# Attention rounds two at a time, the weight fold begun earlier, and copies written in the order of their target

## The chip, the cores and the metric

The kernel runs on one NeuronCore of a Trainium2 chip. The metric is the time of one execution on the device, in microseconds (us). Five engines work side by side, each with its own queue in order: TensorE (matmuls into PSUM), VectorE, ScalarE, GpSimd, and SyncE, whose queue here issues all DMA transfers. A matmul has two rows in a trace: the load of its weights (PEld) and the matmul itself (PE).

## The reference

Inputs come as float64. First an attention with a window: batch 4, 8 heads, 576 tokens, head size 64. Then two MLPs on the 2304 tokens of width 512.

```python
scores = scale * np.matmul(q, k.transpose(0, 1, 3, 2))
rel = pos[:, None] - pos[None, :]
mask_plain = (rel >= 0) & (rel < 32)
mask_dil = (rel >= 0) & (rel < 128) & (rel % 4 == 0)   # heads 4 to 7; heads 0 to 3 have mask_plain
attn = softmax(where(mask, scores, -1e9))
x = (attn @ v) as 2304 x 512
h = x @ w_in; x = maximum(0.01 * h, h) @ w_out         # 512 -> 2048 -> 512
a = x @ w1; b = x @ w2                                 # 512 -> 1024
out = ((a * b) @ w3) @ w_out2                          # 1024 -> 1024 -> 512
```

## The kernel before

**Numbers.** q, k and v are float32; the weights arrive as float64 words, and three engines make float32 of them (`to_float32`, lines 144 to 158: a scaling on a chosen engine, two on ScalarE, a shift and a sum on VectorE). For the MLPs each operand is split in a high and a low part (`split`), and a product is three matmuls (`mm3`, lines 118 to 122).

**Attention.** Two heads make a pair; a pair is worked in two rounds (320 and 256 queries), 8 rounds a batch, 32 in all. A round has these stages. `scores`: per block of 64 queries two 64x64 matmuls against 96 keys, which lie together in the dilated heads because q and k are turned in that order; then scale and mask, the maximum (VectorE), an exponential per block (ScalarE). `normalize`: reciprocal (VectorE) and product (GpSimd). `turn_p`: the probabilities are transposed on TensorE and copied to SBUF by ScalarE. `value_steps`: matmuls with v, then a cast of the result into `x` (ScalarE, line 500) and the low part (VectorE, line 503). In the dilated heads the result goes to every fourth token of `x`. q and k of batch 0 are turned on TensorE and copied by `turn_rows` (line 374), those of batches 1 to 3 on VectorE (`turn_halves`). Two PSUM banks ("side") serve scores, probabilities and values.

**First MLP.** The tokens are in 7 chunks (`CH`), four of 320 or 256 tokens and three of 384. A turn (c, f) is one of 16 slices of 128 hidden columns: `hidden_steps` has 12 matmuls into one of two "h" banks, then a prelu on ScalarE (line 563), which frees the bank, and a split; `project` (12 matmuls) follows two turns later.

**Order.** The first stretch, batches 0 and 1 with the conversion of w_in and w_out and the first 36 turns, stands in an order written out by hand (the string `START`). After it the order of each engine is made by a planner that goes by the program's order and simulated times. There `attention(16, 32)` is a generator, the stream, for batches 2 and 3. After each turn's hidden matmuls `pace` takes some steps of it: 39/28 a turn in chunks 2 and 3, 2.25 a turn from the beginning of chunk 4 (counted from 0) to its turn 13. A round has four steps: `turn_p(n)` with `normalize(n + 1)`; `scores(n + 2)`; the turn of one q or k and a load of another; `value_steps(n)`, after some rounds with a load of v.

**Fold.** At turn 13 of chunk 4 (`LATE`) the rest of the stream is issued, the attention's memory (pool `att`) is closed, and a pool `fold` is opened in its place. `fold_step` converts w_out2 (8 jobs) and w3 (16 jobs) and forms w3 @ w_out2 on TensorE, 1.35 steps a turn through chunk 5. During chunk 6, the last, w1 and w2 are converted, and the product of the fold is loaded back (`load_wp`) and split.

**End.** The second MLP: gates (`gate`) and the last product (`final`).

Of the kernel before, what the change touches and what calls it, by code (L numbers as in the profile page):

```python
# [22 lines left out]
DILATION = 4  # L23
# [5 lines left out]
def tile_window_attention_two_mlps(  # L29
# [70 lines left out]
    def copy_on(e):  # L100
        return e.copy if e is nc.scalar else e.tensor_copy
# [152 lines left out]
    def load_halves(m, src, o):  # L254


        pi, nm = seq[m // 2], "qk"[m % 2]
        t = att.tile([P, NT, D], F32, tag="nat", name=f"{nm}{pi}", bufs=2)
        for g in range(P // E):
            og = o + g // 2 * S * D + g % 2 * E  # L260
            to = t[g * E : (g + 1) * E]
            x = NT * D - E
            nc.sync.dma_start(
                to.rearrange("p n d -> p (n d)")[:, :x], rows(src, og, [[NT * D, E], [1, x]])
            )
        nat_t[nm, pi] = t

    def turn_halves(m):
        pi, nm = seq[m // 2], "qk"[m % 2]
        t = nat_t.pop((nm, pi))  # L270
        dst = att.tile([P, S], F32, tag=nm + "T", name=f"{nm}T{pi}", bufs=2)
        if pair(pi)[2]:
            nc.vector.transpose(dst.rearrange("d (r n) -> d n r", n=NT), t[:, :, :E])
        else:
            for v in range(DILATION):
                us = len(range(v, NT, DILATION))
                other = (NT + v) % DILATION * SR + (NT + v) // DILATION
                to = bass.AP(
                    dst.tensor, dst.offset + v * SR,
                    [list(dst.ap[0]), [1, us], [2 * NT // DILATION, E // 2], [other - v * SR, 2]],  # L280
                )
                at = bass.AP(
                    t.tensor, t.offset + v * D,
                    [list(t.ap[0]), [DILATION * D, us], [2, E // 2], [1, 2]],
                )
                nc.vector.transpose(to, at)
        qk_t[nm, pi] = dst
# [69 lines left out]
    def turn_rows(m):  # L357
        pi, nm = seq[m // 2], "qk"[m % 2]
        plain = pair(pi)[2]
        c = 6 if plain else 8  # L360
        n = S // c
        t = nat_t.pop((nm, pi))
        ps = bank2(f"ps_{nm}T{pi}")
        for g in range(2):
            for c1 in range(c // 2):
                src = t[:n, g * (c // 2) + c1].rearrange("p j d -> p (j d)")
                nc.tensor.transpose(ps[:, g, c1 * n : (c1 + 1) * n], src, ident[:n, :n])
        yield
        dst = att.tile([P, S], F32, tag=nm + "T", name=f"{nm}T{pi}", bufs=2)
        if plain:  # L370
            to = dst.rearrange("d (p g c) -> d g c p", g=2, p=n)
        else:
            to = dst.rearrange("d (c p g) -> d g c p", g=2, p=n)
        copy_on(engine_of[TURN_ON[m]])(to, ps[:, :, : S // 2].rearrange("d g (c p) -> d g c p", p=n))
        qk_t[nm, pi] = dst
        yield

# [2 lines left out]
    def scores(n):  # L380
        if n < NR:
            run(score_steps(n))
# [76 lines left out]
    def value_steps(n):  # L459

        pi, r = order[n]
        b, hp = divmod(pi, HP)
        t = pt.pop(n)
        nb = t.shape[1]
        ps = side_bank(f"ps_o{n}")[:, : nb * QB]
        b, hp = divmod(pi, HP)
        plain = pair(pi)[2]
        vt = v_t[4 * b + 2 * plain + r]
        h = 2 * (hp % (HP // 2))
        for i in range(nb):  # L470
            for j in range(2):
                nc.tensor.matmul(  # L472
                    ps[j * D : (j + 1) * D, i * QB : (i + 1) * QB],
                    vt[i][:, h + j, :],
                    t[:, i, j * QB : (j + 1) * QB],
                    start=True, stop=True,
                )
        yield
        x = xs[hp][:, :, b % 2 * S : (b % 2 + 1) * S]
        views = []  # L480
        s0, s1 = r * HS[0], r * HS[0] + nb * QB
        if plain:
            views.append((x[:, :, s0:s1], ps))
        else:
            spans = []
            for g in range(DILATION):
                j0, j1 = max(0, s0 - g * SR), min(SR, s1 - g * SR)
                if spans and spans[-1][2:] == (j0, j1):
                    spans[-1] = (spans[-1][0], spans[-1][1] + 1, j0, j1)
                elif j0 < j1:  # L490
                    spans.append((g, 1, j0, j1))
            x = x.rearrange("d i (j r) -> d i r j", r=DILATION)
            for g, m, j0, j1 in spans:
                src = bass.AP(
                    ps.tensor, ps.offset + g * SR + j0 - s0,
                    [list(ps.ap[0]), [SR, m], [1, j1 - j0]],
                )
                views.append((x[:, :, g : g + m, j0:j1], src))
        for x, src in views:
            nc.scalar.copy(x[:, 0], src)  # L500
        yield
        for x, src in views:
            nc.vector.tensor_tensor(x[:, 1], src, x[:, 0].bitcast(F32), op=ALU.subtract)
        yield
# [6 lines left out]
    def attention(n0, n1):  # L511

        for m in range(n0, n0 + 4):
            transpose_qk(m)
            load_qk(m + 2)
            if m % 2:
                yield
        load_v(n0 // 2 + 1)
        scores(n0)
        yield  # L520
        scores(n0 + 1)
        normalize(n0)
        yield
        for n in range(n0, n1):
            run(turn_p(n))
            normalize(n + 1)
            yield
            if n % 8 != 3:
                scores(n + 2)
                yield  # L530
            transpose_qk(n + 4)
            load_qk(n + 6)
            yield
            if n % 8 == 3:
                scores(n + 2)
                yield
            run(value_steps(n))
            m = n // NA * 4
            if n % NA in (2, 3):
                load_v(m + n % NA)  # L540
            elif n % NA in (5, 7):
                load_v(m + 4 + (n % NA == 7))
            yield


# [119 lines left out]
    def keep_w3(i):  # L665


        def finish(w, e_hi, e_lo):
            ps = bank(f"ps_w3T{i}")
            for j in range(2):  # L670
                for c in range(NG):
# [1 line left out]
                        ps[:, (j * NG + c) * P : (j * NG + c + 1) * P],  # L673
                        w[:, (c * 2 + j) * P : (c * 2 + j + 1) * P], ident,
                    )
            t = fold.tile([P, 2, 2, NG * P], F32R, tag="w3T", name=f"w3T{i}", bufs=2)
            split(t[:, 0], t[:, 1], ps.rearrange("p (j r) -> p j r", j=2), e_hi, nc.vector)
            w3T.extend((i // (NI // NG), i % (NI // NG) * 2 + j, t[:, :, j]) for j in range(2))

        return finish  # L680

# [23 lines left out]
    wpf = {}  # L705

    def load_wp(ib):
        t = late.tile([P, DM], F32, tag="wpf", name=f"wpf{ib}", bufs=1)
        nc.sync.dma_start(t, wp_dram[ib * P : (ib + 1) * P, :])
        wpf[ib] = t  # L710

# [54 lines left out]

    with ExitStack():
        make_identity(nc, ident)
        att_es, att = pool("att", "right")
# [32 lines left out]

        raw_es, rawp = pool("raw", "left")
        homes = {
            "K": (rawp, "kr", 2), "W": (woB_p, "woB", NF // 2), "N": (att, "nat", 2), "V": (att, "v", 2)
        }
        RAW_AT = "WWWWWWWWWWWWWWWWWWWWWWWWNWNWNWNW"
        PAIR_AT = "KKVVKKVVKKVVKKVVKKVVKKVKVKVKVKVK"
# [99 lines left out]
            if len(todo) > LAG:  # L908
                project(*todo.pop(0))

        LATE = (4, 13)
        FOLD_PACE = 1.35
        wo2_turn = [0]

        def fold_step():
# [13 lines left out]
        stream = attention(2 * NA, NR)  # L929
        owed = [0.0]  # L930

        def begin_fold():
            step(*[stream] * 200)
            att_es.close()
            nonlocal fold, fold_es, conv3
            fold_es, fold = pool("fold", "right")
            jobs = [(load_rows, w_out2, jb, keep_wo2(jb)) for jb in range(NI)]
            jobs += [(load_w3, w3, i, keep_w3(i)) for i in range(NI * NI // NG // 2)]

            def fold_tile(tag, dt, bufs):  # L940
                return lambda i: fold.tile([P, 512], dt, tag=tag, name=f"{tag}f{i}", bufs=bufs)

            conv3 = Convert(
                jobs, fold_tile("raw", U64, 2), fold_tile("w", I32, 2), fold_tile("r", I32, 2),
                FOLD_CONV,
            )
            conv3.fetch(2)

        def pace(c):

            owed[0] += 39 / 28 if c < LATE[0] else 2.25
            while owed[0] >= 1:
                owed[0] -= 1
                step(stream)
# [4 lines left out]
        for c, f0, f1 in runs:  # L959
# [4 lines left out]
            if c == NCH - 1:  # L964
                while conv3.made < len(conv3.jobs) or conv3.done or w3T:
                    fold_step()
                fold_es.close()
                first_es, first_y = pool("first", "right")
                late_es, late = pool("late", "right")

# [95 lines left out]
```

## Time and profile before

| | us |
|---|---|
| timed runs: median (lowest, highest) | 870.29 (866.59, 870.75) |
| the profiled execution, whole | 868.56 |
| its span, first to last instruction | 866.6 |
| TensorE matmuls busy | 848.2 |
| ScalarE busy | 352.6 |
| VectorE busy | 346.7 |
| GpSimd busy | 210.8 |

Busy time counts stretches in which at least one instruction of the engine runs. Matmuls are pipelined, so a matmul's own duration is longer than the distance to the next one; the distance of two starts is what one costs. [...]

### The profile page before, as it was taken

The page shows a single profiled execution, that of the slowest core. Times are in us where ns is not written, and L with a number is a line of the kernel's source. Part 1 is how long each engine was busy: PE and PEld are TensorE (multiplying, and loading weights), DVE is VectorE, ACT ScalarE, POOL GpSimd, SP SyncE. Part 2 cuts the span into 40 slices and gives each one's busy share as a digit, 9 for nine tenths or more (in the row PEclk, how much of TensorE's full clock was granted, in tenths as well). Part 3 has the DMA queues.
Part 4 walks back from the last instruction along what each step waited for, and adds up shares of the span by engine and source line. Part 5 has one row for each costly group of instructions (what it writes and reads, how often), then busy time and mean ns, then how long its engine had stood idle before and what let it go on. Part 6 is the DMA issues. An engine that isn't in the chain of part 4 may idle for free.

```text
span 866.6 us, 14693 instructions
## 1 busy us (share of the span) xinstructions
PE 848.2 (98%) x5774; PEld 772.0 (89%) x5774; DVE 346.7 (40%) x704; ACT 352.6 (41%) x879; POOL 210.8 (24%) x236
## 2 busy tenths in 40 slices
PE   7999998999999999999999999999999999999998
PEld 7799997999999999989899999998888888888887
DVE  4999976344453432274434177731021011000000
ACT  4999945223443343364433175632131121111111
POOL 3311101122322232263222134223123112111110
PEclk9999999999999999999999999999999999999999
DMA  6976575183333311189887575341001000000001
GB/s 152 309 214 231 179 169 137 34 193 73 82 98 92 78 45 50 47 294 349 300 289 236 165 239 155 113 135 49 25 1 61 24 13 13 25 12 13 25 13 48
DMA packets 87333, 103.58 MB, mean 120 GB/s; under 512 B 42849, under 2 KB 65633, under 8 KB 87265
## 3 DMA queue, kind: packets, MB, share of 16 engines
q1 hardware_dynamic: 87264, 102.65, 39.0%
q8 instruction: 45, 0.74, 0.4%
q14 instruction: 24, 0.19, 0.1%
HBM read 85.72 MB, written 16.91 MB: 118 GB/s over the span
## 4 chain that ended last, share of the span: by engine, by line
PE 77%; DMA 7%; DVE 6%; ACT 5%; issue 4%; POOL 2%; SPq 0%; POOLq 0%; DVEq 0%; ACTq 0%
PE ps_ab L120 7%; PE ps_ab L122 7%; PE ps_ab L121 7%; PE ps_x L120 6%; PE ps_x L122 5%; PE ps_x L121 5%; PE ps_h L120 5%; PE ps_h L122 5%; PE ps_h L121 5%; PE ps_y L122 4%; PE ps_y L121 4%; PE ps_y L120 4%; PE ps_s L394 2%; PE ps_o L472 2%; PE ps_wp L122 2%
## 5 line engine op out<-in xcount | busy, mean ns | idle before, releaser
L120 PE MATMUL ps_h<-x,win 128*128 128x384 f32 (+2 forms) x448 | 142.5, 318 | 4.9 <-ACT g L563 4.2
L122 PE MATMUL ps_h<-x,win 128*128 128x384 f32 (+2 forms) x448 | 140.7, 314 | 0.0
L121 PE MATMUL ps_h<-x,win 128*128 128x384 f32 (+2 forms) x448 | 140.4, 313 | 0.0
L120 PE MATMUL ps_x<-gs,wout 128*128 128x384 f32 (+2 forms) x368 | 119.0, 325 | 0.0
L743 DVE TENSOR_TENSOR ab<-a,ps_ab 128x512 f32<-128x512 f32 (+1 forms) x40 | 25.2, 633 | 233.3 <-ACT a L741 225.8
L120 PE MATMUL ps_ab<-ys,w 128*128 128x512 f32 (+1 forms) x320 | 117.7, 368 | 0.6 <-DVE ab L743 0.6
L121 PE MATMUL ps_x<-gs,wout 128*128 128x384 f32 (+2 forms) x368 | 117.7, 320 | 0.1
L122 PE MATMUL ps_ab<-ys,w 128*128 128x512 f32 (+1 forms) x320 | 117.7, 368 | 0.0
L121 PE MATMUL ps_ab<-ys,w 128*128 128x512 f32 (+1 forms) x320 | 117.6, 368 | 0.0
L122 PE MATMUL ps_x<-gs,wout 128*128 128x384 f32 (+2 forms) x368 | 117.4, 319 | 0.0
L112 POOL TENSOR_TENSOR p<-ab,p 128x512 fp32r<-128x512 f32 (+1 forms) x40 | 47.0, 1177 | 211.3 <-ACT p L110 211.3
L110 DVE CAST gs<-g 128x384 fp32r<-128x384 f32 (+2 forms) x92 | 41.3, 449 | 128.9 <-ACT g L563 103.3
L120 PEld LDWEIGHTS ps_h<-x,win 128*128 128x128 f32 x448 | 84.8, 189 | 8.2 <-ACT g L563 6.1
L112 POOL TENSOR_TENSOR gs<-g,gs 128x384 fp32r<-128x384 f32 (+2 forms) x64 | 59.5, 929 | 133.5 <-DVE gs L110 133.5
L563 ACT ACTIVATE g<-ps_h 128x384 f32<-128x384 f32 (+2 forms) x112 | 49.1, 439 | 96.8 <-PE ps_h L122 80.2
L121 PEld LDWEIGHTS ps_h<-x,win 128*128 128x128 f32 x448 | 84.9, 190 | 0.3
L122 PEld LDWEIGHTS ps_h<-x,win 128*128 128x128 f32 x448 | 84.8, 189 | 0.4
L741 ACT COPY a<-ps_ab 128x512 f32<-128x512 f32 (+1 forms) x40 | 21.6, 543 | 139.5 <-PE ps_ab L122 139.5
L120 PEld LDWEIGHTS ps_x<-gs,wout 128*128 128x128 f32 x368 | 69.5, 189 | 1.7
L121 PEld LDWEIGHTS ps_x<-gs,wout 128*128 128x128 f32 x368 | 69.7, 189 | 1.3 <-POOL gs L112 0.4
L122 PEld LDWEIGHTS ps_x<-gs,wout 128*128 128x128 f32 x368 | 69.7, 189 | 0.6
L120 PEld LDWEIGHTS ps_ab<-ys,w 128*128 128x128 f32 x320 | 60.1, 188 | 11.1 <-DVE ab L743 1.0
(109 smaller groups left out, 1553.1 us busy)
## 6 DMA issues: line engine op xcount, KB each, us to landing
wo<-wo_dram SPq DMA_DIRECT2D x32, 512.0 KB
raw<-in_moe_w_in_dram SPq DMA_DIRECT2D x16, 512.0 KB
raw<-in_moe_w_out_dram SPq DMA_DIRECT2D x16, 512.0 KB
rawf<-in_moe_w_dram SPq DMA_DIRECT2D x16, 512.0 KB
raww<-in_moe_w_dram SPq DMA_DIRECT2D x16, 512.0 KB
q<-in_q_dram SPq DMA_DIRECT2D x48, 140.0 KB
k<-in_k_dram SPq DMA_DIRECT2D x48, 140.0 KB
v<-in_v_dram SPq DMA_DIRECT2D x60, 96.0 KB
```

The lines of the kernel that those rows point to most:

```text
L110: copy_on(e_hi)(hi, src)
L112: e_lo.tensor_tensor(lo, src, hi.bitcast(F32), op=ALU.subtract)
L120: nc.tensor.matmul(ps, a[1], b[0], start=first, stop=False)
L121: nc.tensor.matmul(ps, a[0], b[1], start=False, stop=False)
L122: nc.tensor.matmul(ps, a[0], b[0], start=False, stop=last)
L394: nc.tensor.matmul(ps[j * QB : (j + 1) * QB, i - bl.start], qt[d, i * QB : (i + 1) * QB], kt[d, first_key(i, plain) : first_key(i, plain) ...
L472: nc.tensor.matmul(ps[j * D : (j + 1) * D, i * QB : (i + 1) * QB], vt[i][:, h + j, :], t[:, i, j * QB : (j + 1) * QB], start=True, stop=True,)
L563: nc.scalar.activation(g, ps, AF.Prelu, alpha=SLOPE)
L741: nc.scalar.copy(t, ps[0][:, :n])
L743: nc.vector.tensor_tensor(g, t, ps[1][:, :n], op=ALU.mult)
```

## The change

The raw q and k and the turned ones get a pool of their own (`qk`), which stays when `att` is closed. The stream works two rounds at a time: a pass of four steps has `turn_p(n)`; `turn_p(n + 1)` with two turns of q and k; both value steps and the loads of v; both scores with both normalizations. The pace is 22/28 steps a turn, and 14/9 in chunk 4, so that the stream is issued by turn 9 there. The conversion of the fold uses the memory of the raw and turned q and k; it fetches from turn 7 of chunk 4, does a step at turn 10, where the fold's pool is opened, and then goes on with 1.15 steps a turn. The split w3 goes into three halves of a buffer instead of two whole ones. The product that is loaded back in the last chunk gets a second buffer. The copies of q and k in `turn_rows` and of the dilated results in `value_steps` are cut and ordered so that neighbours in the target are written one after the other, and PSUM is read with steps.

```diff
-        dst = att.tile([P, S], F32, tag=nm + "T", name=f"{nm}T{pi}", bufs=2)
+        dst = qkp.tile([P, S], F32, tag=nm + "T", name=f"{nm}T{pi}", bufs=2)
         if plain:
-            to = dst.rearrange("d (p g c) -> d g c p", g=2, p=n)
+            to, dims = dst.rearrange("d (p g c) -> d p g c", g=2, p=n), "d g (c p) -> d p g c"
         else:
-            to = dst.rearrange("d (c p g) -> d g c p", g=2, p=n)
-        copy_on(engine_of[TURN_ON[m]])(to, ps[:, :, : S // 2].rearrange("d g (c p) -> d g c p", p=n))
+            to, dims = dst.rearrange("d (c p g) -> d c p g", g=2, p=n), "d g (c p) -> d c p g"
+        copy_on(engine_of[TURN_ON[m]])(to, ps[:, :, : S // 2].rearrange(dims, p=n))
...
-            spans = []
-            for g in range(DILATION):
-                j0, j1 = max(0, s0 - g * SR), min(SR, s1 - g * SR)
-                if spans and spans[-1][2:] == (j0, j1):
-                    spans[-1] = (spans[-1][0], spans[-1][1] + 1, j0, j1)
-                elif j0 < j1:
-                    spans.append((g, 1, j0, j1))
-            x = x.rearrange("d i (j r) -> d i r j", r=DILATION)
-            for g, m, j0, j1 in spans:
+            x = x.rearrange("d i (j r) -> d i j r", r=DILATION)
+            edges = sorted({0, s0 % SR, s1 % SR, SR})
+            for j0, j1 in zip(edges, edges[1:]):
+                g = [g for g in range(DILATION) if s0 <= g * SR + j0 and g * SR + j1 <= s1]
                 src = bass.AP(
-                    ps.tensor, ps.offset + g * SR + j0 - s0,
-                    [list(ps.ap[0]), [SR, m], [1, j1 - j0]],
+                    ps.tensor, ps.offset + g[0] * SR + j0 - s0,
+                    [list(ps.ap[0]), [1, j1 - j0], [SR, len(g)]],
                 )
-                views.append((x[:, :, g : g + m, j0:j1], src))
+                views.append((x[:, :, j0:j1, g[0] : g[-1] + 1], src))
...
-        scores(n0)
-        yield
-        scores(n0 + 1)
-        normalize(n0)
-        yield
-        for n in range(n0, n1):
+        for n in (n0, n0 + 1):
+            scores(n)
+        yield
+        for n in (n0, n0 + 1):
+            normalize(n)
+        yield
+        for n in range(n0, n1, 2):
             run(turn_p(n))
-            normalize(n + 1)
             yield
-            if n % 8 != 3:
-                scores(n + 2)
-                yield
-            transpose_qk(n + 4)
-            load_qk(n + 6)
+            run(turn_p(n + 1))
+            turn = [lambda m=m: (transpose_qk(m), load_qk(m + 2)) for m in (n + 4, n + 5)]
+            if n % NA != 4:
+                for f in turn:
+                    f()
             yield
-            if n % 8 == 3:
-                scores(n + 2)
-                yield
-            run(value_steps(n))
+            for i in (n, n + 1):
+                run(value_steps(i))
             m = n // NA * 4
-            if n % NA in (2, 3):
-                load_v(m + n % NA)
-            elif n % NA in (5, 7):
-                load_v(m + 4 + (n % NA == 7))
+            if n % NA == 2:
+                load_v(m + 2)
+                load_v(m + 3)
+            elif n % NA in (4, 6):
+                load_v(m + 2 + n % NA // 2)
+            yield
+            for i in (n + 2, n + 3):
+                scores(i)
+            if n % NA == 4:
+                for f in turn:
+                    f()
+            for i in (n + 2, n + 3):
+                normalize(i)
             yield
...
-            t = fold.tile([P, 2, 2, NG * P], F32R, tag="w3T", name=f"w3T{i}", bufs=2)
-            split(t[:, 0], t[:, 1], ps.rearrange("p (j r) -> p j r", j=2), e_hi, nc.vector)
-            w3T.extend((i // (NI // NG), i % (NI // NG) * 2 + j, t[:, :, j]) for j in range(2))
+            for j in range(2):
+                t = fold.tile([P, 2, NG * P], F32R, tag="w3T", name=f"w3T{i}_{j}", bufs=3)
+                split(t[:, 0], t[:, 1], ps[:, j * NG * P : (j + 1) * NG * P], e_hi, nc.vector)
+                w3T.append((i // (NI // NG), i % (NI // NG) * 2 + j, t))
...
-        t = late.tile([P, DM], F32, tag="wpf", name=f"wpf{ib}", bufs=1)
+        t = late.tile([P, DM], F32, tag="wpf", name=f"wpf{ib}", bufs=2)
...
-        LATE = (4, 13)
-        FOLD_PACE = 1.35
+        LATE = (4, 10)
+        CONV_AT = (4, 7)
+        FOLD_PACE = 1.15
...
+        def begin_conv():
+            nonlocal conv3
...
+            def words(tag, dt):
+                return lambda i: qkp.tile([P, 512], dt, tag=tag, name=f"{tag}f{i}", bufs=2)
+
+            conv3 = Convert(jobs, words("nat", U64), words("qT", I32), words("kT", I32), FOLD_CONV)
+            conv3.fetch(2)
...
-            owed[0] += 39 / 28 if c < LATE[0] else 2.25
+            owed[0] += 22 / 28 if c < LATE[0] else 14 / 9
...
+                if (c, f) == CONV_AT:
+                    begin_conv()
                 if (c, f) == LATE:
+                    conv3.step()
                     begin_fold()
```

## Rows read from the trace of the kernel before

**Rows 1.** The page's first part: busy us, share, instructions of each engine.
```profile
PE 848.2 (98%) x5774; PEld 772.0 (89%) x5774; DVE 346.7 (40%) x704; ACT 352.6 (41%) x879; POOL 210.8 (24%) x236
```

**Rows 2.** Busy time by stretch: length; PE, PEld, DVE, ACT, POOL; clock, DMA share, GB/s.
```profile
20.00:40.00 20.00, 18.19 (x262) 15.51 (x263) 18.65 (x45) 18.26 (x67) 7.34 (x9) 1.00 1.05 313
...
385.40:388.70 3.30, 3.30 (x12) 3.30 (x11) 3.16 (x4) 1.56 (x3) 2.76 (x3) 0.50 0.98 315
...
198.00:361.00 163.00, 163.00 (x1516) 153.62 (x1515) 61.61 (x155) 62.38 (x239) 45.28 (x52) 1.00 0.28 69
361.00:400.00 39.00, 36.82 (x204) 36.11 (x203) 24.73 (x35) 24.29 (x41) 22.35 (x23) 0.96 0.80 283
400.00:500.00 100.00, 100.00 (x535) 91.15 (x534) 37.17 (x63) 35.51 (x61) 20.57 (x26) 1.00 0.77 259
500.00:580.00 80.00, 78.16 (x471) 76.37 (x470) 53.05 (x87) 46.29 (x86) 28.39 (x30) 1.00 0.50 154
```

**Rows 3.** TensorE's matmuls in order of time: start us, duration us, instruction.
```profile
177.50 0.31 PE L122 MATMUL ps_x<-gs,wout 128*128 128x320 f32 x1
177.74 1.54 PE L394 MATMUL ps_s<-kT,qT 64*64 64x96 f32 x32
179.20 0.42 PE L120 MATMUL ps_x<-gs,wout 128*128 128x320 f32 x1
...
202.50 0.88 PE L394 MATMUL ps_s<-kT,qT 64*64 64x96 f32 x16
203.30 0.42 PE L120 MATMUL ps_h<-x,win 128*128 128x320 f32 x1
203.56 0.31 PE L121 MATMUL ps_h<-x,win 128*128 128x320 f32 x1
203.70 0.31 PE L122 MATMUL ps_h<-x,win 128*128 128x320 f32 x1
...
213.43 1.04 PE L394 MATMUL ps_s<-kT,qT 64*64 64x96 f32 x20
214.40 0.80 PE L472 MATMUL ps_o<-pT,v 96*64 96x64 f32 x20
215.13 0.41 PE L121 MATMUL ps_h<-x,win 128*128 128x320 f32 x1
```

**Rows 4.** All engines in order of time around 382 us; in brackets idle before and releaser.
```profile
379.12 1.47 POOL L112 TENSOR_TENSOR gs<-g,gs 128x384 fp32r<-128x384 f32 x1
379.64 1.24 DVE L141 TENSOR_SCALAR wf<-wf 128x512 int32<-128x512 int32 x1
...
381.85 0.41 DVE L141 TENSOR_SCALAR wf<-wf 128x512 int32<-128x512 int32 x1
381.96 0.62 ACT L110 CAST wo<-wf 128x512 fp32r<-128x512 f32 x1 [2.70 <-DVE wf L157]
...
383.74 0.47 ACT L563 ACTIVATE g<-ps_h 128x384 f32<-128x384 f32 x1
...
384.26 0.19 PEld L120 LDWEIGHTS ps_h<-x,win 128*128 128x128 f32 x1 [2.37 <-ACT g L563]
```

**Rows 5.** VectorE by form (busy us, mean ns), and line 374's copies (ns min/median/max).
```profile
L503 DVE TENSOR_TENSOR x<-ps_o,x 128x288 fp32r<-128x288 f32 x8 | 5.5, 688 | 0.9 <-ACT x L500 0.6
...
L503 DVE TENSOR_TENSOR x<-ps_o,x 128x320 fp32r<-128x320 f32 x8 | 3.9, 488 | 1.0 <-ACT x L500 0.9
...
L503 DVE TENSOR_TENSOR x<-ps_o,x 128x32 fp32r<-128x32 f32 x8 | 1.7, 208 | 0.0
...
L374 DVE COPY qT<-ps_qT x3: 757/1176/1198, 6.6 to 23.4; 128x576 f32<-128x576 f32 x3
```

**Rows 6.** ScalarE by form: exponentials, copies of probabilities, output copy; busy us, mean ns.
```profile
L418 ACT ACTIVATE s<-s,nmax 128x96 f32<-128x96 f32 x144 | 52.1, 364 | 38.8 <-DVE nmax L414 37.3 <-DVE total L430 1.3
...
L455 ACT COPY pT<-ps_p 96x384 f32<-96x384 f32 x32 | 15.3, 480 | 9.0 <-PE ps_p L451 8.6
...
L500 ACT CAST x<-ps_o 128x288 fp32r<-128x288 f32 x8 | 5.4, 676 | 9.2 <-PE ps_o L472 9.2
```

More of the change, by code (lines that the diff above doesn't have):

```diff
@@ L257, in load_halves @@
         pi, nm = seq[m // 2], "qk"[m % 2]
-        t = att.tile([P, NT, D], F32, tag="nat", name=f"{nm}{pi}", bufs=2)
+        t = qkp.tile([P, NT, D], F32, tag="nat", name=f"{nm}{pi}", bufs=2)
         for g in range(P // E):
@@ L368, in turn_rows @@
         yield
-        dst = att.tile([P, S], F32, tag=nm + "T", name=f"{nm}T{pi}", bufs=2)
+        dst = qkp.tile([P, S], F32, tag=nm + "T", name=f"{nm}T{pi}", bufs=2)
         if plain:
-            to = dst.rearrange("d (p g c) -> d g c p", g=2, p=n)
+            to, dims = dst.rearrange("d (p g c) -> d p g c", g=2, p=n), "d g (c p) -> d p g c"
         else:
-            to = dst.rearrange("d (c p g) -> d g c p", g=2, p=n)
-        copy_on(engine_of[TURN_ON[m]])(to, ps[:, :, : S // 2].rearrange("d g (c p) -> d g c p", p=n))
+            to, dims = dst.rearrange("d (c p g) -> d c p g", g=2, p=n), "d g (c p) -> d c p g"
+        copy_on(engine_of[TURN_ON[m]])(to, ps[:, :, : S // 2].rearrange(dims, p=n))
         qk_t[nm, pi] = dst
@@ L768, in tile_window_attention_two_mlps @@
         make_identity(nc, ident)
+        qkp_es, qkp = pool("qk", "right")
         att_es, att = pool("att", "right")
@@ L804, in tile_window_attention_two_mlps @@
         homes = {
-            "K": (rawp, "kr", 2), "W": (woB_p, "woB", NF // 2), "N": (att, "nat", 2), "V": (att, "v", 2)
+            "K": (rawp, "kr", 2), "W": (woB_p, "woB", NF // 2), "N": (qkp, "nat", 2), "V": (att, "v", 2)
         }
@@ L930, in tile_window_attention_two_mlps @@
         owed = [0.0]
+        def begin_conv():
+            nonlocal conv3
+            jobs = [(load_rows, w_out2, jb, keep_wo2(jb)) for jb in range(NI)]
+            jobs += [(load_w3, w3, i, keep_w3(i)) for i in range(NI * NI // NG // 2)]
+            def words(tag, dt):
+                return lambda i: qkp.tile([P, 512], dt, tag=tag, name=f"{tag}f{i}", bufs=2)
+            conv3 = Convert(jobs, words("nat", U64), words("qT", I32), words("kT", I32), FOLD_CONV)
+            conv3.fetch(2)
         def begin_fold():
@@ L934, in begin_fold @@
             att_es.close()
-            nonlocal fold, fold_es, conv3
+            nonlocal fold, fold_es
             fold_es, fold = pool("fold", "right")
[L937 to L947, printed above, removed]
         def pace(c):
-            owed[0] += 39 / 28 if c < LATE[0] else 2.25
+            owed[0] += 22 / 28 if c < LATE[0] else 14 / 9
             while owed[0] >= 1:
@@ L967, in tile_window_attention_two_mlps @@
                 fold_es.close()
+                qkp_es.close()
                 first_es, first_y = pool("first", "right")
```

## The prediction

> **What bounds the kernel now.** The page's first part comes first: TensorE is busy 98% of the span, every other engine under 42% [rows 1]. So an edit counts only if it takes idle time or slow matmuls from TensorE; the change adds and removes no matmul. The second view is the busy time by stage [rows 2]: from 198 to 361 us (the stream, batches 2 and 3 between the first MLP's turns) TensorE shows no idle time at all, from 361 to 400 us (the fold begins) 39.00 - 36.82 = 2.2 us, from 500 to 580 us (last chunk of the first MLP) 1.8 us, from 20 to 40 us 1.8 us. The reader is to see that the stages differ: in the first 40 us VectorE and ScalarE are at 18 of 20 us, later nobody but TensorE is full. The third view is TensorE's instructions in order of time, because a busy share hides what a busy engine loses between matmuls [rows 3].
>
> **Two rounds at a time.** A 320-column matmul follows the last after 0.14 us (203.56 to 203.70) [rows 3]. Where 64x64 score matmuls follow, the gap is 177.74 - 177.50 = 0.24, so 0.09 more; the first matmul after them takes 203.56 - 203.30 = 0.26, so 0.11 more. In between, 32 score matmuls of two rounds in a row took 179.20 - 177.74 = 1.46, a single round of 16 took 203.30 - 202.50 = 0.80: two singles cost 0.14 more than a double. A group that joins its neighbour thus saves 0.09 + 0.11 + 0.14 = 0.34 us. Value groups look alike (20 of them took 215.13 - 214.40 = 0.73), and I take 0.34 for them too (from 0.14, the part inside the group alone, to 0.34). The stream has 16 rounds, so 16 score and 16 value groups; in the new loop scores n+2 and n+3 stand side by side, and values n and n+1 too, which takes away 8 and 8: 16 x 0.34 = 5.4 at most. Two deductions. Three times a score group already stands right before a value group, as at 213.43 and 214.40, which saves a way out and a way in, 0.2 each time, 0.6 now. And the planner must leave the pairs together. In chunks 2 and 3 the pace is 22/28 steps a turn, so a whole turn of MLP lies between two steps and both rounds' inputs and both side banks are ready: 22 - 4 steps are 4.5 passes of four steps, 9 groups removed for certain. In chunk 4 the pace is 14/9, 4 steps in 2.6 turns, and value steps may be pulled apart because the second round's probabilities come later; I count half of the other 7. That is (9 + 3.5) x 0.34 - 0.6 = 3.6. **Stream: -3.6 us** (from -4.8, all merged, to +0, none). Transposes of probabilities get no price: they go in and out of the stream of wide matmuls without a visible gap.
>
> **What else moves in the stream.** The pair's nine exponentials are one burst on ScalarE, 9 x 0.36 = 3.3 us [rows 6], where a round had four or five. Behind them in ScalarE's queue waits the next prelu, and behind that hidden(f+2). Cover: TensorE has two projections and the other "h" bank, 36 matmuls, at 256 columns about 0.147 x 256/320 = 0.12 each: 4.3 us. So nothing, as long as nothing else joins the burst (the slower rival below). The q/k turn of a pair puts two transposes together on VectorE, which is busy 62 of 163 us in this stretch [rows 2]; loads of v for two rounds are issued together, on SP, with the 16 DMA engines at 0.28 [rows 2], one pass of four steps (15 to 22 us) ahead of use. Both nothing; without the cover a late transpose would hold the scores of one pair, not the MLP.
>
> **The fold's beginning.** Here is the one large loss. At 382 us TensorE's weight load waits 2.37 us for a prelu (384.26) [rows 4]. That prelu (383.74) stood in ScalarE's queue behind a cast that waited 2.70 us for VectorE, and VectorE was late because its shift took 1.24 us beside a GpSimd subtract, where the same shift took 0.41 at 381.85. [...] It fell in the conversion of w_out2, the jobs that use GpSimd twice, just as chunk 4's ends were evacuated. After the change the first two loads and one conversion are issued from turn 7 and at turn 10, the pace drops from 1.35 to 1.15, and chunk 4's evacuation comes six to seven jobs further on, near the end of the eight w_out2 jobs. The same queue order can bite again (nothing takes it away), but in a thinner stretch. **Fold's beginning: -3.0 us**, from -3.9 (gone) to +3.9 (twice). The number of steps stays: 22 turns x 1.15 = 25 and one at turn 10, against 19 x 1.35 = 25. New: 16 more casts and 16 more subtracts, because w3T is split in halves. The least instruction of this kind takes 0.21 us [rows 5], so 16 x 0.2 = 3.3 us on each engine, hidden in 100 us of which ScalarE uses 36 and VectorE 37 [rows 2]. Three half buffers instead of four make the second half of each job wait for a product of the one before; bounds 0 to 15 x 0.21 = 3.2 us, I take 0 because TensorE has that product ready and next in order.
>
> **Copies along their target.** The subtract into every fourth element takes 688 ns for 288 elements, the straight one 488 ns for 320 [rows 5]; the q/k copy with 8-byte steps takes 757 ns, with 24-byte steps 1176 to 1198. So a target with steps of 16 bytes and more costs about double. The new order writes runs; but it reads PSUM with steps of 288 to 2048 bytes, which no row of before does. Bounds: if the read is free, four plain q/k copies save 0.45 each on VectorE (1.8 us) and the dilated output copies some 0.2 a round on each engine. These lie in the hand-written start, whose first 40 us are bound by VectorE and ScalarE together; ScalarE gains only its own 0.6, and later stalls in batch 1 some 0.4. If the read costs what the write costs now, nothing is gained there and the dilated q/k copies, two on VectorE and two on ScalarE, get 0.42 dearer in the chain that starts the kernel: +1.7. **Start: -0.7 us** (-2.5 to +1.7); I take the free read: every slow copy there [rows 5] writes with steps of 16 bytes or more, and the one that writes denser isn't slow. [...]
>
> **The last chunk.** Two wpf buffers instead of one let the next load go early; TensorE's idle time there is 1.8 us [rows 2], and what precedes it on ScalarE is mostly the weight conversion, not this load. **-0.3 us** (-1.5 to +0.5).
>
> **Sum.** -3.6 - 3.0 - 0.7 - 0.3 = -7.6. The profiled execution took 868.56 us (span 866.6 and 2.0 around it): 861.0. The timed runs of before have a median of 870.29, 1.7 above it, and the lowest is 866.59; the profiled one lies between them, so after may read 861.0 to 862.7. I say 862.
>
> **Rivals.**
> 1. *The gains are halved* (22%). The planner pulls the pairs apart, or the stall at the fold's start comes back one chunk end later. For it: the order of every engine after the start is the planner's, and ScalarE's queue still holds prelus behind conversions. Against: before, single groups stay whole (20 or 16 in one piece). Time: the pairs alone -7.6 + 3.6 = -4.0, 864.6; the stall alone -4.6, 864.0; both -1.0, 867.6; each up to 1.7 more by the median. I say 866.5.
> 2. *Slower: the burst meets its copies* (14%). Place: ScalarE in the stream. If the pair's probability copies (0.48 for three blocks, so some 0.75 a round) and output copies (0.68 for the long piece) [rows 6] fall into the exponentials, 3.3 + 1.5 + 1.4 = 6.2 us lie before a prelu that has 4.3 us of cover: 1.9 us idle, like the stall at 382, with the slow clock behind it (1.7): 3.6 a pair. At two pairs the gain is gone; at four it is 868.56 - 7.6 + 14.4 = 875.4. For it: the stall at 382 shows the mechanism. Against: in the stream of before ScalarE has such neighbours without one idle microsecond of TensorE, and the planner knows ScalarE's load.
> 3. *Stepped reads of PSUM cost what stepped writes do* (13%): -7.6 + 0.7 + 1.7 = -5.2, 863.4 to 865.1.
> 4. The forecast (51%): 859 to 865.5, its own range.
>
> **How the numbers follow.** A measurement of this kernel tells a difference of 0.5%, 4.35 us on 870.29: faster is under 865.9, slower over 874.6. Faster: the forecast nearly whole (0.47), the third rival (0.11), little of the first: 0.58 to 0.60. Slower: most of the second rival, 0.11. Same: the rest, 0.30. Range for 8 in 10: 857 (all bounds of the stream and the start good) to 871 (the first rival, and the second at two or three pairs).
>
> **What would show it.** In TensorE's order of time, groups of 32 to 40 score and value matmuls, under 22 of both kinds together between the first score and the last value, and no idle time there; the stream ending near 345 us instead of 361. From there to 400 us, TensorE idle under 1 us and no stretch at granted clock 0.50. The q/k copies of the plain pairs under 0.8 us, the long output copy under 0.5. Wrong would be: groups of 16 and 20 still; a prelu that TensorE waits for in the stream; q/k copies over 1.1 us for the dilated pairs too; a wait of the w3T casts for the fold's products.

## The result and the profile after

| | before | after |
|---|---|---|
| timed runs: median (lowest, highest), us | 870.23 (866.59, 870.75) | 880.49 (878.87, 882.09) |
| ratio after to before, 95% interval | | 1.0127 (1.0094 to 1.0160) |
| the profiled execution, its span, us | 868.56, 866.6 | 880.39, 878.3 |

The kernel became 1.3% slower where 1% faster was forecast. The page's first part looks as before [rows 1]: TensorE's busy time is even 1.4 us less, its share falls from 98 to 96%. So the loss is idle time, and the place is asked from the stages.

```profile
PE 846.8 (96%) x5774; PEld 774.3 (88%) x5774; DVE 337.1 (38%) x720; ACT 350.9 (40%) x895; POOL 208.1 (24%) x236
```

Busy time by stretch in the kernel after (length; PE, PEld, DVE, ACT, POOL; granted clock, DMA share, GB/s), to be laid beside [rows 2]:

```profile
198.00:361.00 163.00, 163.00 (x1514) 157.98 (x1514) 62.38 (x159) 65.58 (x243) 47.46 (x55) 1.00 0.29 76
361.00:400.00 39.00, 24.66 (x151) 23.09 (x150) 16.19 (x30) 17.72 (x33) 14.61 (x16) 0.78 0.65 228
...
382.70:399.80 17.10, 7.02 (x22) 6.52 (x23) 7.67 (x14) 9.06 (x16) 5.13 (x6) 0.50 0.97 350
400.00:500.00 100.00, 96.87 (x514) 86.75 (x513) 34.32 (x77) 36.94 (x78) 23.49 (x28) 1.00 0.75 256
500.00:580.00 80.00, 80.00 (x461) 79.48 (x461) 53.68 (x87) 43.19 (x77) 23.25 (x27) 1.00 0.47 148
```

From 361 to 400 us TensorE idles 39.00 - 24.66 = 14.3 us, where it was 2.2; the other engines are no fuller than before, all under 18 of 39 us. From 400 to 500 us there are 3.1 us that before did not have, from 500 to 580 us the 1.8 us of before are gone. The stretch at half clock grew from 3.3 to 17.1 us.

The stream hides its gain in such a table, because TensorE is busy in both. It shows where the same work is measured between two fixed matmuls: from the first score of the stream to the first hidden matmul of chunk 5's turn 1, the traces of both kernels have the same 1,593 matmuls. (Turns are counted below from chunk 4's first as 0; chunk 4 has 16, so this one is turn 17.) TensorE in order of time, before (start, duration):

```profile
198.69 1.04 PE L394 MATMUL ps_s<-kT,qT 64*64 64x96 f32 x20
...
359.31 0.34 PE L472 MATMUL ps_o<-pT,v 96*64 96x64 f32 x4
...
375.81 0.33 PE L120 MATMUL ps_h<-x,win 128*128 128x384 f32 x1
...
395.01 0.60 PE L672 MATMUL ps_w3T<-ident,wf 128*128 128x128 f32 x4
```

And after, with some of the groups between:

```profile
199.05 1.04 PE L394 MATMUL ps_s<-kT,qT 64*64 64x96 f32 x20
...
217.60 1.27 PE L472 MATMUL ps_o<-pT,v 96*64 96x64 f32 x36
222.36 1.70 PE L394 MATMUL ps_s<-kT,qT 64*64 64x96 f32 x36
...
327.89 1.87 PE L394 MATMUL ps_s<-kT,qT 64*64 64x96 f32 x40
...
345.80 1.39 PE L472 MATMUL ps_o<-pT,v 96*64 96x64 f32 x40
350.79 1.54 PE L394 MATMUL ps_s<-kT,qT 64*64 64x96 f32 x32
...
370.21 1.15 PE L472 MATMUL ps_o<-pT,v 96*64 96x64 f32 x32
...
371.75 0.34 PE L120 MATMUL ps_h<-x,win 128*128 128x384 f32 x1
```

Three terms make up the span's 11.7 us: until the first score +0.4 (199.05 - 198.69); the stream -4.4 (172.70 instead of 177.12); all that follows +15.8 (506.55 instead of 490.79). All groups but the first two scores have 32 to 40 matmuls, 17 groups from 199 us on. But the last values stand at 370.2, right before turn 17, where before had its last at 359.3 and its first transposes of w3 (`w3T`) only at 395.0. The changed program issues these last values by turn 9.

TensorE around the stall of after (in brackets idle before and what ended it):

```profile
378.22 0.34 PE L122 MATMUL ps_x<-gs,wout 128*128 128x384 f32 x1
383.48 0.69 PE L120 MATMUL ps_x<-gs,wout 128*128 128x384 f32 x1 [4.92 <-ACT st L636]
...
387.16 0.52 PE L122 MATMUL ps_x<-gs,wout 128*128 128x384 f32 x1
396.98 1.11 PE L674 MATMUL ps_w3T<-ident,qTf 128*128 128x128 f32 x4 [9.30 <-DVE qTf L157]
397.75 0.67 PE L120 MATMUL ps_h<-x,win 128*128 128x384 f32 x1
```

Two waits, 4.9 and 9.3 us, and the second is new in kind: the transposes of w3, the fold's first matmuls, stand in TensorE's queue ahead of turn 18's hidden matmuls, and the converted words that they read (`qTf`) aren't there yet. What holds them is seen in ScalarE's queue:

```profile
371.68 1.14 ACT L110 CAST wo<-qTf 128x512 fp32r<-128x512 f32 x2
...
377.80 0.62 ACT L110 CAST wo<-qTf 128x512 fp32r<-128x512 f32 x1 [1.66 <-DVE qTf L157]
...
379.93 0.79 ACT L151 ACTIVATE kTf<-natf 128x512 f16<-128x512 f32 x1 [0.50 <-DMA natf<-in_moe_w_out_dram]
...
381.71 0.79 ACT L151 ACTIVATE kTf<-natf 128x512 f16<-128x512 f32 x1 [0.36 <-DMA natf<-in_moe_w_out_dram]
382.36 0.74 ACT L153 ACTIVATE kTf<-natf 128x512 int16<-128x512 uint32 x1
382.97 0.45 ACT L636 COPY st<-ps_x 128x384 f32<-128x384 f32 x1
...
387.96 0.78 ACT L151 ACTIVATE kTf<-natf 128x512 f16<-128x512 f32 x1 [3.08 <-DMA natf<-in_moe_w_out_dram]
...
391.73 0.62 ACT L110 CAST wo<-qTf 128x512 fp32r<-128x512 f32 x1 [0.59 <-DVE qTf L157]
...
394.80 0.78 ACT L151 ACTIVATE kTf<-natf 128x512 f16<-128x512 f32 x1 [2.46 <-DMA natf<-in_moe_w_dram]
```

The eight casts of w_out2 (`wo`) begin at 371.68, right behind the stream's last output cast, and end at 391.7; two jobs of w3 follow. Two buffers of raw words make the jobs go by twos, 5.5 to 7.2 us a pair (pairs of `wo` casts begin at 371.7, 377.8, 383.3 and 390.5). The copy of the chunk's result out of PSUM (`st`, 382.97), for which the first wait of TensorE was, stands behind two conversions that waited for their loads. SyncE's issues show the loads of the pairs, 374.88 and 381.42, 5.1 and 6.5 us before ScalarE goes on with them:

```profile
374.88 1.17 SPq L132 DMA_DIRECT2D natf<-in_moe_w_out_dram  x2
...
381.42 2.08 SPq L132 DMA_DIRECT2D natf<-in_moe_w_out_dram  x2
...
389.43 1.65 SPq L649 DMA_DIRECT2D natf<-in_moe_w_dram  x2
```

The copies became faster, on VectorE and ScalarE (busy us, mean ns), beside [rows 5, 6]:

```profile
L374 DVE COPY kT<-ps_kT 128x576 f32<-128x576 f32 x3 | 2.3, 753 | 2.6 <-PE ps_kT L367 2.6
...
L498 DVE TENSOR_TENSOR x<-ps_o,x 128x224 fp32r<-128x224 f32 x16 | 6.1, 383 | 0.0
...
L498 DVE TENSOR_TENSOR x<-ps_o,x 128x96 fp32r<-128x96 f32 x8 | 2.1, 257 | 8.5 <-ACT x L495 8.2 <-PE ps_p L451 0.3
...
L495 ACT CAST x<-ps_o 128x224 fp32r<-128x224 f32 x16 | 5.8, 364 | 0.0
```

### The profile page after: what moved, and what is told of

It reads as the page before. It is cut to its first block, busy times and chain, and to the rows that moved or that the text cites. A ratio compares the mean times of both kernels' runs of the same rounds, so it can differ in the third digit from the quotient of the medians.

```text
span 878.3 us, 14750 instructions
## 1 busy us (share of the span) xinstructions
PE 846.8 (96%) x5774; PEld 774.3 (88%) x5774; DVE 337.1 (38%) x720; ACT 350.9 (40%) x895; POOL 208.1 (24%) x236
## 4 chain that ended last, share of the span: by engine, by line
PE 78%; issue 6%; DMA 5%; DVE 4%; ACT 4%; POOL 1%; SPq 0%; POOLq 0%; DVEq 0%; ACTq 0%
PE ps_ab L120 7%; PE ps_ab L122 7%; PE ps_ab L121 7%; PE ps_x L120 6%; PE ps_x L122 6%; PE ps_x L121 6%; PE ps_h L120 6%; PE ps_h L122 6%; PE ps_h L121 6%; PE ps_y L120 4%; PE ps_y L122 4%; PE ps_y L121 4%; PE ps_s L394 3%; PE ps_o L472 2%; PE ps_p L451 1%
## 5 line engine op out<-in xcount | busy, mean ns | idle before, releaser
L112 POOL TENSOR_TENSOR p<-ab,p 128x512 fp32r<-128x512 f32 (+1 forms) x40 | 47.0, 1176 | 210.4 <-ACT p L110 210.4
L110 DVE CAST gs<-g 128x384 fp32r<-128x384 f32 (+2 forms) x92 | 34.1, 371 | 139.4 <-ACT g L565 116.8
```

Source lines behind the costliest of these rows:

```text
L110: copy_on(e_hi)(hi, src)
L112: e_lo.tensor_tensor(lo, src, hi.bitcast(F32), op=ALU.subtract)
```

## The experiments

Every kernel is the one after with the edit shown. The table gives for each: the time (one run, or the median and ratio to before on the same chip); the start of the stream's first score; from there to turn 17's first hidden matmul; from there to the end of the span; the records of matmuls on TensorE between the last values and the first w3T; and the waits over 0.3 us that TensorE had for `st` and for w3T's words from 361 to 420 us. (With single rounds and the early fold, e3, the first w3T stands before turn 17, so two columns can't be compared.)

| run | us (ratio, 95%) | first score | to turn 17 | rest | matmuls | waits |
|---|---|---|---|---|---|---|
| before | 870.23 | 198.69 | 177.12 | 490.8 | 181 | 0 |
| after | 880.49 (1.0127) | 199.05 | 172.70 | 506.6 | 50 | 14.2 |
| e1_fold_turn13 | 870.53 | 198.71 | 172.70 | 497.0 | 98 | 9.7 |
| e2b_fold_turn17 | 861.11 (0.9931) | 198.41 | 172.70 | 487.6 | 160 | 0.6 |
| e3_single_rounds | 869.1 | 197.91 | - | - | 139 | 3.2 |
| e5_old_copies | 883.56 | 200.02 | 172.69 | 508.7 | 50 | 14.8 |
| e7_stream_faster | 877.14 | 196.02 | 172.69 | 506.3 | 50 | 16.8 |
| e8_fold_turn17_pace2 | 863.5 (0.9947) | 196.55 | 172.70 | 490.2 | 146 | 4.1 |
| e9_fold_turn17_old_copies | 861.09 (0.9929) | 196.28 | 172.69 | 488.9 | 160 | 1.2 |
| e10_no_normalize | 868.8 | 199.09 | 172.65 | 495.1 | 118 | 3.9 |
| e12_fold_two_paces | 863.43 (0.9953) | 196.48 | 172.70 | 491.2 | 164 | 0.9 |
| e13_one_wpf | 880.65 | 197.76 | 172.70 | 508.1 | 50 | 15.3 |
| e14_fold_turn17_single | 866.0 (0.9976) | 197.81 | 176.85 | 489.9 | 253 | 0 |

**The fold three turns later.**

```diff
-        LATE = (4, 10)
-        CONV_AT = (4, 7)
-        FOLD_PACE = 1.15
+        LATE = (4, 13)
+        CONV_AT = (4, 10)
+        FOLD_PACE = 1.35
```

> The changed kernel with the fold's three numbers as before (pool at turn 13 of chunk 4, first loads at turn 10, 1.35 steps a turn); all else stays. Theory A (the stream really ends at turn 17 of TensorE's order and not at turn 9, the fold's first writes wait for its memory, and eight conversions must then fit before the first w3 transposes, whose place in TensorE's order is fixed at turn 18): the place moves 2 turns of 4.15 us later, to turn 20, so the 14.7 us of idle time shrink to about 6 and the time falls to 869 to 873 us. Rival B (the fold's loads through two buffers are too slow wherever it starts): the idle time stays at 14 us or more, 879 to 883 us.

It took 870.53 against 866.66 for before on the same chip. The stream ends at the same place; the first w3T moves two turns on, to turn 20, and 98 matmuls instead of 50 lie before it. TensorE's waits from 361 us on:

```profile
PE ps_w3T L674 <- DVE qTf L157: 7.8, 2, 7.0
PE ps_x L120 <- ACT st L636: 1.9, 1, 1.9
```

48 more matmuls at 0.17 are 8.3 us of cover; the waits fell by 4.5 and the rest of the kernel by 9.6. The direction is that of the theory that the fold begins too early for its words; the place was still too early.

**The fold at turn 17, where the stream really ends.**

```diff
-        LATE = (4, 10)
+        LATE = (5, 1)
-        FOLD_PACE = 1.15
+        FOLD_PACE = 25 / 15
...
-            owed[0] += 22 / 28 if c < LATE[0] else 14 / 9
+            owed[0] += 22 / 28 if c < 4 else 14 / 9
```

> The changed kernel with the fold's pool opened at turn 1 of chunk 5 (17 turns after the beginning of chunk 4) and 25/15 steps a turn, so that all steps still fit; first loads at turn 7 as in the changed kernel. Theory A: the first w3 transposes stand near turn 23, 20 us after the stream's end, and the idle time at 378 to 397 us goes to 0 to 4 us; 862 to 867 us. Rival B: steps at 2.5 us each outrun loads that take 3.5 us, so the idle time is spread over the fold and the time stays at 875 us or more.

One run: 861.4, before 866.66. Timed again in several runs:

> The kernel of e2 (pool of the fold opened 17 turns after the beginning of chunk 4, 25/15 steps a turn), timed against before: 0.990 to 0.996 of it, if the stall at the fold's beginning was the whole loss and the stream's gain stays.

861.11 (860.41 to 861.96) against 867.59 (865.74 to 871.76), ratio 0.9931 (0.9914 to 0.9947): faster than before. Waits from 361 us on, then the first w3T on TensorE, then busy time by stretch:

```profile
PE ps_x L120 <- ACT st L636: 0.6, 1, 0.6
...
399.58 0.63 PE L674 MATMUL ps_w3T<-ident,qTf 128*128 128x128 f32 x4
...
361.00:402.00 41.00, 40.22 (x258) 38.98 (x257) 20.02 (x32) 19.28 (x37) 20.70 (x21) 1.00 0.64 220
402.00:480.00 78.00, 77.98 (x413) 69.56 (x412) 31.84 (x70) 34.52 (x68) 17.21 (x22) 1.00 0.89 312
```

The last values stand where they stood, the eight conversions are no quicker (29.1 us from the last values to the first w3T, 25.8 in after), but 160 matmuls lie between, and no wait for the words is left. The halves of w3T and the two buffers of words are the same in this kernel, so a theory that blames them falls.

**Single rounds in the stream.**

```diff
-        for n in range(n0, n1, 2):
-            run(turn_p(n))
...
+        for n in range(n0, n1):
+            run(turn_p(n))
+            normalize(n + 1)
...
-            owed[0] += 22 / 28 if c < LATE[0] else 14 / 9
+            owed[0] += 39 / 28 if c < LATE[0] else 2.9
```

> The changed kernel with the attention loop of before (one round at a time; 39/28 steps a turn, then 2.9 so that the stream is issued by turn 10), fold and copies as changed. Theory A with its cause in the pairs (each step of a pass waits for both side banks, so that a pass of two rounds takes four to five turns): single rounds end near turn 12 or 13, the conversions get 4 to 5 turns before turn 18, the idle time falls under 5 us; the stream pays 4 to 5 us for its singles: 867 to 873 us. Rival C (the fold's early loads and conversions by themselves, not the pairs, make the stall): idle time stays over 12 us, 882 us or more.

869.1. The stream is over at 353.5 us, before turn 12, and the `wo` casts begin at 354.06: they follow the last values within 0.6 us here as in after. 139 matmuls lie before the first w3T, and one wait is left there, for `st`:

```profile
PE ps_x L120 <- ACT st L629: 3.2, 1, 3.2
```

So it was the pass of two rounds that moved the stream's end five turns back. The gain of the pairs is lost too, and at 577 us TensorE waits 2.0 us for a gate of the second MLP.

**Copies in the order of before.**

```diff
-            to, dims = dst.rearrange("d (p g c) -> d p g c", g=2, p=n), "d g (c p) -> d p g c"
+            to = dst.rearrange("d (p g c) -> d g c p", g=2, p=n)
...
-            x = x.rearrange("d i (j r) -> d i j r", r=DILATION)
+            x = x.rearrange("d i (j r) -> d i r j", r=DILATION)
```

> The changed kernel with the copies of q, k and the dilated results in the order of before. Theory D (the faster copies bring the start's chain to a GpSimd scaling that waits 3.5 us for a weight load, and the clock falls after it): the first hidden matmul, at 39.8 us in the changed kernel, starts at 38.7 as before, and there is no stretch at half clock near 31 us; the total is 0.5 to 1.5 us lower. Rival: the start differs from execution to execution by its loads, and the first hidden matmul stays within 0.3 us of 39.8.

883.56, no better than after, and neither value came: the first hidden matmul starts at 41.2 us, later than in after (39.8), and the half clock of the start lies at 38.9 to 42.3 us instead of 31.1 to 34.6. The start varies from one execution to the next more than the copies could move it: the first score of the stream lies between 196.0 and 199.1 us in eleven runs with the new copies, at 196.3, 198.7 and 200.0 in three with the old ones (before among them).

**The stream issued twice as fast in chunk 4.**

```diff
-            owed[0] += 22 / 28 if c < LATE[0] else 14 / 9
+            owed[0] += 22 / 28 if c < LATE[0] else 14 / 4.5
```

> The changed kernel with 14/4.5 stream steps a turn in chunk 4, so that the program issues the stream by turn 5 instead of turn 9; all else as changed. If the stream's end is set by the chain of a pass (scores, exponentials, transposes, values, each of which waits for the two side banks of the one before), it stays at turn 16 to 17, the idle time at 378 to 397 us too, 877 to 883 us. If it is set by where the program issues the steps, the end moves to turn 13 or 14 and the time falls to 862 to 872 us.

877.14 in one run, with the first score 3.0 us earlier than in after and the rest as long as there (506.3 and 506.6). The last groups keep their distances to a hundredth (compare 345.80, 350.79 and 370.21):

```profile
342.77 1.39 PE L472 MATMUL ps_o<-pT,v 96*64 96x64 f32 x40
347.76 1.54 PE L394 MATMUL ps_s<-kT,qT 64*64 64x96 f32 x32
...
367.18 1.15 PE L472 MATMUL ps_o<-pT,v 96*64 96x64 f32 x32
```

In chunk 4 the place where the program issues the stream's steps does not decide where TensorE does them.

**The stream without the product that normalizes.** In batches 2 and 3 the probabilities are not divided by their sums.

```diff
-        nc.gpsimd.tensor_tensor(
-            s, s, rec[:, :nb].unsqueeze(2).to_broadcast([P, nb, KB]), op=ALU.mult
-        )
+        if n < 2 * NA:
+            nc.gpsimd.tensor_tensor(
+                s, s, rec[:, :nb].unsqueeze(2).to_broadcast([P, nb, KB]), op=ALU.mult
+            )
```

> The changed kernel without GpSimd's product of probabilities and reciprocals in batches 2 and 3 (0.83 to 0.99 us a round in the chain of a pass; these batches are then not divided by their sums). If a pass is held by the chain from scores to transposes, the 1.6 turns between them shrink, the stream ends at turn 15 to 16 instead of 17 and the idle time at 378 to 397 us falls by some 4 to 8 us (870 to 877 us). If it is held by the steps that wait for the side banks of the step before (transposes, transposes, values, scores: 2.4 turns of a pass), it ends at 16.5 to 17 and the time stays over 876 us.

868.8, a little better than expected. The stream's end moves from turn 17 to turn 14:

```profile
334.50 1.39 PE L473 MATMUL ps_o<-pT,v 96*64 96x64 f32 x40
339.48 1.54 PE L394 MATMUL ps_s<-kT,qT 64*64 64x96 f32 x32
...
356.31 1.15 PE L473 MATMUL ps_o<-pT,v 96*64 96x64 f32 x32
```

From the last scores to the last values it takes 16.8 us instead of 370.21 - 350.79 = 19.4. So this product, which lies between scores and transposes, is on the chain that sets the length of a pass, 20.4 us here (319.05 to 339.48) and 22.9 in after (327.89 to 350.79). The other parts of that chain were not taken out one by one. With 118 matmuls before w3T the one wait over 0.5 us is again for `st`, 3.9 us.

**The fold at turn 17 and quicker, two ways.**

```diff
-        FOLD_PACE = 1.15
+        FOLD_PACE = 2.0
```

> As e2, with 2.0 fold steps a turn, so that the fold ends about two turns earlier. In e2 the last chunk again has waits for preludes of 1.9 us in 520 to 560 us, in the changed kernel 0.0. If these come from the fold ending late (turn 33 in e2, 31 in the changed kernel), they go, 1 to 2 us under e2; rival: the loads can't follow (1.5 MB a w3 step), waits for w3 transposes and preludes at 400 to 480 us add 2 us or more.

863.5 (ratio 0.9947, 0.9923 to 0.9970): missed, it was to be 1 to 2 us under the fold at turn 17, and the two intervals overlap. Its edit of `LATE` and of the chunks' pace is that of the fold at turn 17. The fold ends at turn 30 instead of 33, and TensorE's idle time from 500 to 580 us falls from 0.7 to 0.3. But w3T stands one turn earlier, and the wait is back:

```profile
PE ps_w3T L674 <- DVE qTf L157: 3.2, 2, 2.0
PE ps_x L120 <- ACT st L636: 0.9, 1, 0.9
```

The other way kept the slow pace for the eight conversions only:

```diff
-                    owed[0] += FOLD_PACE
+                    owed[0] += 1.4 if conv3.made < NI + 1 else 2.0
```

> As e2 (fold's pool 17 turns after the beginning of chunk 4), with 1.4 steps a turn for the eight w_out2 conversions and 2.0 after them. The first w3 transposes then stand near turn 23.5, the idle time at 380 to 400 us goes under 1.5 us, and the fold ends before turn 32, so that the waits for preludes in the last chunk (1.9 us in e2) go as in the kernel with 2.0 throughout: 859 to 861 us, 0.2 to 2 us under e2.

863.43 (ratio 0.9953, 0.9935 to 0.9971): missed. The beginning is clean with 164 matmuls, but from 402 to 480 us w3T's transposes now wait for a prelu that frees their bank, behind conversions:

```profile
PE ps_w3T L674 <- ACT g L565: 2.9, 2, 2.3
```

**The fold at turn 17 with the copies of before.** The edits of the second and the fourth experiment together.

> As e2, with the copies of q, k and the dilated results in the order of before. If the faster copies shorten the start (VectorE saves 1.7 us, ScalarE 0.6 in it), this is 0.5 to 1.5 us slower than e2; if the start is set by the weight loads' landing, the same within 0.5 us.

861.09 (ratio 0.9929, 0.9906 to 0.9952) against 861.11 with the new order on the same chip. The copies do differ (ns min, median, max), so what they gain does not show in the time:

```profile
L374 DVE COPY kT<-ps_kT x3: 759/1186/1187, 8.9 to 25.7; 128x576 f32<-128x576 f32 x3
```

**One buffer for the fold's product.**

```diff
-        t = late.tile([P, DM], F32, tag="wpf", name=f"wpf{ib}", bufs=2)
+        t = late.tile([P, DM], F32, tag="wpf", name=f"wpf{ib}", bufs=1)
```

> The changed kernel with one buffer for the loaded product in the last chunk, as before. If the last chunk's gain (TensorE loses 0.0 us in 520 to 560 us, 2.2 before) comes from the fold's earlier end, it stays under 0.3 us; if it comes from the second buffer, 1.5 to 2.2 us are lost there again.

880.65, as after, and the last chunk of the first MLP stays without idle time, so the second buffer isn't what took the 1.8 us:

```profile
500.00:580.00 80.00, 80.00 (x460) 79.48 (x459) 45.86 (x87) 43.74 (x80) 24.01 (x27) 1.00 0.48 148
```

What goes with it is the turn at which the fold ends: 31 in after and here, 32.4 in before, where 1.8 us are idle, 33 in the fold at turn 17, where 0.7 are. The turn alone doesn't give the size.

**The fold at turn 17 with single rounds.** The edits of the second and the third experiment together; the stream is over before turn 12.

> As e2, with the attention loop of before (one round at a time, 39/28 and then 2.9 steps a turn). TensorE loses 11.4 us between matmuls from 160 to 360 us, as before and in e3, against 6.8 in e2: 4 to 5 us slower than e2, 865 to 866 us. Rival: the pairs' gain is given back elsewhere in e2 and both are the same within 1 us.

866.0 (ratio 0.9976, 0.9964 to 0.9987). From the first score to turn 17, the same 1,593 matmuls, and the first `wo` cast between:

```profile
197.81 1.04 PE L394 MATMUL ps_s<-kT,qT 64*64 64x96 f32 x20
...
353.96 1.15 ACT L110 CAST wo<-qTf 128x512 fp32r<-128x512 f32 x2
...
374.66 0.34 PE L120 MATMUL ps_h<-x,win 128*128 128x384 f32 x1
```

176.85 us, before's 177.12 and not the pairs' 172.70. The pairs are worth 4.2 us, and the two ratios (0.9976 and 0.9931, each against before on its own chip) say 0.45%, 3.9 us. The `wo` casts begin within 0.6 us of the last value matmul here too, though the program opens the fold's pool only at turn 17.

## Why the prediction was wrong

**The step that failed** is the fold's beginning, and in it the sentence that "the same queue order can bite again (nothing takes it away), but in a thinner stretch". -3.0 was put down, with +3.9 as the worst. After turn 17 the kernel lost 15.8 us, and the last chunk had given 1.8 back: +17.6 for the fold. It comes in four pieces: 12.2 more idle from 361 to 400 us (14.3 and 2.2), 3.1 from 400 to 500 us, the half clock on 22 matmuls (7.02 us, at 0.17 each 3.7, so 3.3, where before paid 1.2 to 1.7), and 0.2 to 0.7 that I can't place. No run shows the 3.9 that bounds the term, or the 1.7 that the slower rival adds for the clock, as such: before's trace has the wait of 2.37 us [rows 4] and, after it, 12 matmuls in 3.30 us at a granted clock of 0.50 [rows 2], where twelve took 2.08 us right before the wait (379.79 to 381.87); that is 1.2 us more, or 1.65 as half of the 3.30.

Two things behind that step were wrong. First, I read the places from the program: the stream "ending near 345 us", the conversions begun at turn 10. The trace has the last values at 370 us, before turn 17, because a pass of two rounds takes 22.9 us, about four and a half turns, and not the 2.6 turns at which chunk 4 issues one. With twice the issue pace nothing moved; without the normalizing product the end moved three turns. The trace of before has the rows to see this by: there the stages follow one another with about a turn of MLP between (scores at 276.9 us, values at 280.7, transposes at 284.3, scores at 287.8).

Second, I priced the conversion as work on VectorE and ScalarE, and looked for the wait that before had had. TensorE's own wait for the conversion's result has no term in the sum. Before had none either, only because 181 matmuls, about 31 us, stood between the last values (359.3) and the first w3T (395.0). After has 50, about 9 us, because `LATE` moved to turn 10 and the stream's end to turn 17. The transposes did not move with the stream's end: they belong to the tenth step of the conversion, and one step at turn 10 and 1.15 a turn make that turn 17, right ahead of turn 18's hidden matmuls. The same count gives turn 20 for before, 19 with the fold three turns later, 22 for the fold at turn 17 and 21 with 2.0 steps a turn, and each trace has them behind that turn's hidden matmuls. The `wo` casts write into memory that the attention used before, and in every changed kernel the first one starts within 0.6 us of the last value matmul, wherever that lies: at 371.7 us in after, 354.1 with single rounds, 357.8 without the product. From that matmul to the first w3T it takes 25.8 to 29.8 us in all runs but before and the last one, and cover and wait add up: 50 matmuls leave 14.2 to 16.8 us of waits, 98 leave 9.7, 118 to 146 leave 3 to 4, 160 and 164 leave 0.6 to 1.2. The part of them that is for `st` comes from the same queue (the copy out of PSUM behind conversions that wait for their loads). Whether more buffers of words would shorten the chain itself was not tried.

**Stream, -3.6:** right. -4.4 in after, 4.2 between the single and the double rounds. All pairs held together, 7 groups of scores and 8 of values in one piece each, so the upper estimate, -4.8, was the nearer one. The burst of exponentials cost TensorE nothing: it is without idle time from 198 to 361 us, and the slower rival, which put the loss there, is out. The place of the loss stood in the first rival, but as the old stall come back (864.0 us), not as this wait.

**Start, -0.7:** the copies became faster as forecast, but no saved time is seen. A q/k copy that reads PSUM with steps is as quick as the fastest of before (757 ns): the plain ones fell from 1176 to 1198 ns to 745 to 758, and a low part of 128x224 takes 383 ns where 128x288 took 688. The third rival is out. Writing with wide steps costs 1.6 times here, not about double: in the trace of the fold at turn 17 with the old copies it is 1178 to 1189 ns with targets of 24-byte steps, 759 with 8-byte steps. In time the copies are worth nothing that can be measured, 861.09 and 861.11.

**Last chunk, -0.3:** -1.8 in after, -1.2 in the fold at turn 17, by another cause than the one given. One buffer does as well. With 2.0 steps a turn the fold ended earlier and the idle time fell from 0.7 to 0.3 us, so the fold's earlier end is the likely cause; no run separates it from the rest.

**The sum:** -7.6 was forecast. The fold at turn 17 comes near it: span 858.7 instead of 866.6, that is -0.3 at the start, -4.4 in the stream and -3.2 behind it, -7.9. That compares two executions on different chips; timed beside before on one chip, its ratio of 0.9931 (0.9914 to 0.9947) is 4.6 to 7.5 us. The stall at 382 us of before is gone there, as forecast. So most of what the change was forecast to give is in it, and its place and pace for the fold took back 19.0 us (506.6 - 487.6).

## What to carry to other kernels

Where work is moved to an earlier place in the program, take from the trace when its inputs are really done, and count the matmuls of the bottleneck engine between that point and the first one that needs the result; where that cover is shorter than the chain between them, the difference is a wait, however free the engines of the chain are. Here the place of that first one could be counted from the program, in steps of the conversion; the place of the inputs could not. A group of stages that is made longer ends later, and what is queued to begin behind it (here a pool in its memory) moves with it. Measure a gain in a busy stretch between two fixed instructions with the same work between, not by busy shares.

## Of the hardware, not expected

Reading PSUM with a step between elements cost VectorE and ScalarE nothing that these runs show: 753 ns for 576 elements on VectorE, against 757 ns for the copy of before that read in order and wrote with 8-byte steps, and 638 ns on ScalarE, against 680 and 697. In the wait of 4.9 us the granted clock fell to 0.50 at 382.7 us, and it stayed there through twelve matmuls 0.32 us apart, the wait of 9.3 us and the matmuls behind it, until 399.8; in the fold at turn 17, with no wait over 0.6 us, it was 1.00 from 361 to 480 us.
